# An attention block with modulation on one core: scale mods as rows, batch-1 transposes ahead of V, row-tiled text keys, output weights in row chunks

## The chip, the cores and the metric

One core of a Trainium2 chip. The metric is the device time of one execution in microseconds; lower is better. It is about 1.8 us more than the span of the profile, which starts and ends with the program's own instructions. The kernel before took 121.41 us (median of 3 runs, 121.23 to 121.57). A difference is called faster or slower from 2% on.

## The reference

Two token streams, image (2 x 256 tokens) and text (2 x 32), of width D = 1152, are normalised, modulated by vectors made from `c`, attended over jointly with one head of width D, projected and gated:

```python
mod_i = (_silu(c) @ wmod_img).reshape(B, 6, 1, D)      # shift, scale, gate are used; the same for text
hi = _layernorm(x_img) * (1 + sci) + shi               # ht likewise
qkvi, qkvt = hi @ wqkv_img, ht @ wqkv_txt
q, k, v = [concatenate([text, image], axis=1)]         # 288 tokens per batch
p = _softmax(einsum('bqd,bkd->bqk', q, k) * D ** -0.5)
a = einsum('bqk,bkd->bqd', p, v)
out_i = x_img + gai * (ai @ wo_img)                    # out_t likewise
```

Each of the 14 weight blocks is 1152 x 1152 in bf16, 2592 KB.

## The kernel before

The parts that the change touches; cuts are marked with `...`. `P` is 128, `KT` is 9 (rows of 128 of a weight block), `NTOK` is 288. TensorE runs its matmuls in the order of the program, as the chain of waits in the prediction shows. A **dummy** is a matmul whose result is never read.

```python
    for r0, r1 in ((0, 1), (1, 3), (3, 6), (6, KT)):              # V's weights, rows in four pieces
        nc.sync.dma_start(w_v_i[:, r0:r1, :], v_v[:, r0:r1, :])
    ...
    w_o_i = load_w(3, wo_img, 0)                                   # one DMA for the whole block
    ...
    def warm_up(n):                                                # dummies: their result is never read
        for _ in range(n):
            mm(wps[:], lhsT=warm[:, 0:P], rhs=warm[:], start=True, stop=True)
    warm_up(8)
    ...                                                            # transposes of silu(c)
    warm_up(17)
    ...
    def sc_cols(r0, r1):                                           # scale of the image, as columns
        ...
        for kt in range(r0, r1):
            for j in range(KT):
                mm(sc_ps[:, j, :], lhsT=w_sc_i[:, kt, j * P:(j + 1) * P], rhs=sT[:, kt, :], ...)
    ...                                                            # x normalised, 18 transposes of batch 0
    sc_cols(0, 4)
    warm_up(5)
    sc_cols(4, 7)
    out01 = x_transposes(0, 1)                                     # six transposes of batch 1
    sc_cols(7, K8)
    sc_cols(K8, KT)
    out31 = x_transposes(3, 1)
    out01()
    x_scale(0, 3, 0, sc_ps)                                        # VectorE, scale read from PSUM
    ...
    v_open(A0, 0, 3)                                               # V, four accumulators, rows 0 to 2
    out61 = x_transposes(6, 1)
    ...
    v_open(A1, 0, 3)
    v_open(A0 + A1, 3, KT - 2)
    ...
    def attn_out(b, d0=0, d1=KT):
        for dt in range(d0, d1):
            aps = ps_mm.tile([P, NTOK], f32, tag="mm")             # six PSUM buffers
            for kj in range(3):                                    # two blocks of image keys, one of text
                lhsT = v_i[...] if kj < 2 else v_t[...]            # text: 64 of 128 rows are zeros
                mm(aps[:], lhsT=lhsT, rhs=pT[:, kj, :], start=(kj == 0), stop=(kj == 2))
            ...                                                    # eviction, VectorE and ACT in turn

    v_txt()
    scores_txt()
    scores_img(0)
    img_gate()
    scores_img(1)
    p_transposes(0)
    txt_gate()
    attn_out(0, 0, 5)
    p_transposes(1)
    attn_out(0, 5, KT)
    attn_out(1)
```

## Time and profile before

| | before |
|---|---|
| time, median of 3 | 121.41 us |
| span of the profile | 119.5 us |
| TensorE busy | 114.6 us (96%) |
| DMA | full from 3 to 98.6 us |

The page's main lines and the chain of waits stand in the prediction. One more line of that chain serves below as the **mark** at which the front of the kernel is over, the first matmul of the image shift, which follows 63 matmuls of V (columns: start, length, what):

```profile
28.89 1.22 PE gps L61 x36
```

### The profile page before, as it was taken

Reading aid. Unit: us, or ns where it says so; the run is one execution under the profiler, and the core shown is the slowest. Engines: PE = TensorE matmul, PEld = TensorE weight load, DVE = VectorE, ACT = ScalarE, POOL = GpSimd, SP = SyncE. Lnnn points to the kernel's source line nnn. Section 1 sums busy time; section 2 is a strip of 40 time slices with the busy share of each in tenths; the row PEclk is TensorE's granted clock in tenths of the full one; section 3 lists DMA queues with packets and bytes.
Section 4 is the critical chain, followed back from the end, with each engine's and each line's share of the span. In section 5 each row is a group of like instructions: output and inputs, shape, how many; then the busy total and the mean of one; then the engine's idle time right before and its main releaser. Section 6 shows DMA issues by size and latency. Waiting matters only on the chain.

```text
span 119.5 us, 2609 instructions
## 1 busy us (share of the span) xinstructions
PE 114.6 (96%) x1105; PEld 67.2 (56%) x1105; DVE 74.1 (62%) x155; ACT 42.2 (35%) x86; POOL 11.6 (10%) x34
## 2 busy tenths in 40 slices
PE   5999999999999999999999999999999999999980
PEld 2248754445574444445444467886777866567660
DVE  1678292053866899999999700017785756666670
ACT  5799402031761424323039132335347610000000
POOL 8240000000000000000000000000211807100000
PEclk9999999999999999999999999999999999999999
DMA  3999999999999999999999999999999992620222
GB/s 136 379 383 396 403 404 411 415 408 414 405 398 400 401 413 411 411 413 410 415 403 410 413 413 411 406 411 405 413 417 397 411 370 81 148 99 0 99 68 80
DMA packets 18517, 40.86 MB, mean 342 GB/s; under 512 B 923, under 2 KB 1451, under 8 KB 18507
## 3 DMA queue, kind: packets, MB, share of 16 engines
q1 hardware_dynamic: 17632, 39.56, 84.9%
q0 software_dynamic: 480, 0.89, 2.5%
q10 hardware_dynamic: 395, 0.26, 0.7%
q8 instruction: 8, 0.13, 0.4%
q14 instruction: 2, 0.02, 0.0%
HBM read 39.38 MB, written 1.34 MB: 341 GB/s over the span
## 4 chain that ended last, share of the span: by engine, by line
PE 95%; DVE 2%; issue 0%; DVEq 0%
PE ps L61 52%; PE vps L61 15%; PE wps L61 8%; PE aps L61 6%; PE gps L61 6%; PE sps L61 4%; PE sc_ps L61 2%; PE tp L64 1%; PE pT_ps L64 1%; DVE tmp L615 1%; DVE o L616 0%; PE tpt L64 0%; DVE hS_i L240 0%; DVE warm L128 0%; PE sT_ps L64 0%
## 5 line engine op out<-in xcount | busy, mean ns | idle before, releaser
L61 PE MATMUL ps<-xT_i,t 128*128 128x512 bf16 x162 | 35.8, 379 | 0.0
L61 PEld LDWEIGHTS <-t 128*128 128x128 bf16 x405 | 22.8, 98 | 19.4 <-issue 0.7
L398 DVE SCALAR_TENSOR_TENSOR acc_sh<-t,sTf,acc_sh 128x1152 f32<-128x1152 bf16 x16 | 21.3, 1405 | 0.0
L61 PE MATMUL ps<-t,aT 128*128 128x384 bf16 (+3 forms) x153 | 20.2, 308 | 0.0
L61 PE MATMUL vps<-t,hS_i 128*128 128x512 bf16 (+1 forms) x108 | 18.1, 326 | 0.1
L61 PEld LDWEIGHTS <-aT 128*128 128x128 bf16 (+1 forms) x153 | 13.0, 101 | 7.1 <-issue 0.5
L61 PEld LDWEIGHTS <-hS_i 128*128 128x128 bf16 x108 | 8.9, 98 | 8.6 <-DVE hS_i L240 0.3
L61 PE MATMUL wps<-warm 128*128 128x512 bf16 x30 | 9.8, 491 | 1.2 <-DVE warm L128 1.2
L615 DVE TENSOR_TENSOR tmp<-ps,gb 128x384 bf16<-128x384 f32 (+2 forms) x13 | 6.8, 526 | 6.4 <-PE ps L61 5.2
L348 ACT ACTIVATE qkT<-ps 128x512 bf16<-128x512 f32 (+2 forms) x11 | 6.2, 563 | 12.3 <-PE ps L61 12.3
L483 POOL DMA_DIRECT2D mod_scratch<-g_sb x4 | 2.5, 634 | 78.3 <-ACT g_sb L173 78.3
L350 ACT CAST qkT<-ps 128x512 bf16<-128x512 f32 (+2 forms) x11 | 5.9, 554 | 8.5 <-PE ps L61 8.5
L171 DVE CAST v_i<-vps 128x512 bf16<-128x512 f32 x5 | 3.5, 692 | 7.6 <-PE vps L61 7.6
L171 DVE CAST v_t<-ps 64x288 bf16<-64x288 f32 x2 | 0.9, 460 | 11.7 <-ACT v_t L173 11.7
L61 PE MATMUL aps<-pT,v_i 128*128 128x288 bf16 x36 | 6.7, 287 | 0.0
L61 PEld LDWEIGHTS <-warm 128*128 128x128 bf16 x30 | 3.3, 117 | 5.9 <-issue 3.3
L587 DVE TENSOR_SCALAR aT<-aps,svc 128x288 bf16<-128x288 f32 x9 | 4.7, 518 | 2.4 <-PE aps L61 2.3
L61 PE MATMUL sps<-qkT 128*128 128x288 bf16 (+1 forms) x54 | 5.5, 287 | 0.0
L589 ACT ACTIVATE aT<-aps,svc 128x288 bf16<-128x288 f32 x9 | 4.5, 501 | 2.5 <-PE aps L61 2.5
L61 PE MATMUL aps<-pT,v_t 128*128 128x288 bf16 x18 | 5.1, 286 | 0.0
L61 PE MATMUL gps<-t,sT 128*32 128x288 bf16 x144 | 5.1, 287 | 0.0
L61 PE MATMUL ps<-hT_t,t 128*128 128x64 bf16 x162 | 5.1, 193 | 0.0
(106 smaller groups left out, 108.8 us busy)
## 6 DMA issues: line engine op xcount, KB each, us to landing
t<-in_wqkv_txt_dram SPq DMA_DIRECT2D x3, 2592.0 KB, 15.9
t<-in_wmod_img_dram SPq DMA_DIRECT2D x2, 2592.0 KB, 17.0
t<-in_wqkv_img_dram SPq DMA_DIRECT2D x2, 2592.0 KB, 20.3
t<-in_wmod_txt_dram SPq DMA_DIRECT2D x2, 2592.0 KB, 15.0
t<-in_wmod_txt_dram SPq DMA_DIRECT2D x3, 864.0 KB, 16.2
t<-in_wo_img_dram SPq DMA_DIRECT2D x1, 2592.0 KB
t<-in_wo_txt_dram SPq DMA_DIRECT2D x1, 2592.0 KB, 20.1
t<-in_wqkv_img_dram SPq DMA_DIRECT2D x2, 864.0 KB, 13.9
```

Source lines behind the costliest of these rows:

```text
L61: return pin(nc.tensor.matmul(*a, **k))
L64: return pin(nc.tensor.transpose(*a, **k))
L171: nc.vector.tensor_copy(out_ap, in_ap)
L348: nc.scalar.mul(out_ap, in_ap, SCALE)
L350: nc.scalar.copy(out_ap, in_ap)
L398: pin(eng.scalar_tensor_tensor(acc[:, b, :], w[:, kt, :], sTf[:, kt, b:b + 1], acc[:, b, :], op0=ALU.mult, op1=ALU.add))
L483: nc.gpsimd.dma_start(gsc[si, b, :].rearrange("(g j) -> g j", g=NGG), g_sb[b:P:32, :])
L587: nc.vector.tensor_scalar(dst, aps[:], bias, None, op0=ALU.add)
L589: nc.scalar.activation(dst, aps[:], ACT.Identity, bias=bias)
L615: nc.vector.tensor_mul(tmp[:, 0:n], ps[:, 0:n], gb[:, b, c0:c0 + n])
```

## The change

Its intent: take dummies off TensorE's path, let V start without transposes in between, have the text keys of two output tiles run side by side, let text V cover the softmax, and let the output projection start on part of its weights. `tile_position` makes a matmul use a part of TensorE's 128 x 128 array, here 32 columns or 64 rows of it; going from one such division to another is a change of **tiling mode**. The scale is said below to be in **column form** before the change and in **row form** after it.

```diff
-    for r0, r1 in ((0, 1), (1, 3), (3, 6), (6, KT)):
+    for r0, r1 in ((0, 1), (1, 2), (2, 3), (3, 5), (5, 7), (7, KT)):
...
-    w_o_i = load_w(3, wo_img, 0)          # and w_o_t
+    w_o_i = load_rows(3, wo_img, 0)       # three DMAs each
...
-    nc.vector.memset(warm[:], 0.0)
+    nc.vector.memset(warm[:], 1.0)
...
-    warm_up(17)
+    warm_up(14)
...
-            for j in range(KT):
-                mm(sc_ps[:, j, :], lhsT=w_sc_i[:, kt, j * P:(j + 1) * P], rhs=sT[:, kt, :], ...)
+            for g in range(NGG):          # four 32-column tiles, 288 columns each
+                mm(sc_ps[LW * g:LW * g + LW], lhsT=sT32[:, kt, :], rhs=group(w_sc_i, kt, g), ...,
+                   tile_position=(0, LW * g))
...
-    sc_cols(0, 4); warm_up(5); sc_cols(4, 7)
+    sc_rows(0, 4); warm_up(3); sc_rows(4, 7); warm_up(1)
...
+    sc1_i = mod_cols_of(sc_ps, "scc")     # VectorE's 32x32 block transpose
     out01()
-    x_scale(0, 3, 0, sc_ps)
+    x_scale(0, 3, 0)
+    out61 = x_transposes(6, 1)
     v_open(A0, 0, 3)
-    out61 = x_transposes(6, 1)
...
+        nc.vector.tensor_copy(v_t[64:64 + NTT, :], v_t[0:NTT, :])     # text V a second time
...
+    def attn_pair(ids0, ids1):            # two groups of three output tiles
+        attn_keys(t0, True)               # image keys of the first group
+        for n, key in enumerate(...):     # six text matmuls, t0 and t1 in turn
+            r0 = 64 * (n % 2)
+            mm(..., lhsT=v_t[r0:r0 + 64, ...], rhs=pTs[b][r0:r0 + 64, 2, :],
+               start=first, stop=not first, tile_position=(r0, 0))
+        attn_evac(t0); attn_keys(t1, False); attn_evac(t1)
...
-    v_txt()
     scores_txt(); scores_img(0); img_gate(); scores_img(1)
+    v_txt()
     p_transposes(0); txt_gate()
-    attn_out(0, 0, 5); p_transposes(1); attn_out(0, 5, KT); attn_out(1)
+    attn_pair(G[0], G[1]); p_transposes(1); attn_pair(G[2], G[3]); attn_pair(G[4], G[5])
```

More of the change, by code (lines that the diff above doesn't have):

```diff
@@ L120 @@
     w_ga_t = load_w(2, wmod_txt, 2 * D)
-    w_o_i = load_w(3, wo_img, 0)
-    w_o_t = load_w(1, wo_txt, 0)
+    w_o_i = load_rows(3, wo_img, 0)
+    w_o_t = load_rows(1, wo_txt, 0)
     nc.scalar.preload_act_table_set("natural_log_exp_and_others")
@@ L127 @@
     warm = const.tile([P, 512], bf)
-    nc.vector.memset(warm[:], 0.0)
-    unit = const.tile([P, P + B * KT], bf)
-    nc.gpsimd.memset(unit[:, 0:P], 1.0 / P)
-    nc.gpsimd.memset(unit[:, P:], 1.0)
+    nc.vector.memset(warm[:], 1.0)
+    NGG = 4
+    LW = P // NGG
+    unit = const.tile([P, LW], bf)
+    nc.vector.memset(unit[:], 1.0 / P)
     ident = const.tile([P, P], bf)
@@ L207, with group, mod_cols_of, sc_rows @@
     xT_i = act.tile([P, KT, B * NI], bf)
-    sc1_i = const.tile([P, KT, B], f32)
     qkT = act.tile([P, 2 * KT, B, NTOK], bf, tag="Q")
-    sc_ps = ps_mm.tile([P, KT, B], f32, tag="mm")
-    def sc_cols(r0, r1):
+    def group(w, kt, g):
+        return w[:, kt, :].rearrange("p (c g l) -> p g c l", g=NGG, l=LW)[:, g]
+    def mod_cols_of(gps, name):
+        t = const.tile([P, KT, LW], f32, name=name, tag={"shtc": "scc", "sctc": "shc"}.get(name, name))
+        pin(nc.vector.transpose(t[:].rearrange("p c l -> p (c l)"), gps[:].rearrange("p c l -> p (c l)")))
+        return t
+    sc_ps = ps_mm.tile([P, KT, LW], f32, tag="mm")
+    def sc_rows(r0, r1):
         if r0 == 0:
-            mm(sc_ps[:].rearrange("p kt b -> p (kt b)"), lhsT=unit[:, 0:P], rhs=unit[:, P:],
-               start=True, stop=False, skip_group_check=True)
+            for g in range(NGG):
+                mm(sc_ps[LW * g:LW * g + LW].rearrange("p c l -> p (c l)"), lhsT=unit[:], rhs=warm[:, 0:KT * LW],
+                   start=True, stop=False, tile_position=(0, LW * g))
         for kt in range(r0, r1):
-            for j in range(KT):
-                mm(sc_ps[:, j, :], lhsT=w_sc_i[:, kt, j * P:(j + 1) * P], rhs=sT[:, kt, :],
-                   start=False, stop=(kt == KT - 1), skip_group_check=True)
+            for g in range(NGG):
+                mm(sc_ps[LW * g:LW * g + LW], lhsT=sT32[:, kt, :], rhs=group(w_sc_i, kt, g),
+                   start=False, stop=(kt == KT - 1), tile_position=(0, LW * g))
     def x_transposes(k0, b):
@@ L235, in x_transposes, with x_scale @@
         return copy_out
-    def x_scale(k0, k1, b, sc=None):
-        sc = sc1_i if sc is None else sc
+    def x_scale(k0, k1, b):
         for kt in range(k0, k1):
             pin(nc.vector.tensor_scalar(hS_i[:, kt, b * NI:(b + 1) * NI], xT_i[:, kt, b * NI:(b + 1) * NI],
-                                        sc[:, kt, b:b + 1], None, op0=ALU.mult))
+                                        sc1_i[:, kt, b:b + 1], None, op0=ALU.mult))
     VW = 512
@@ L280 @@
         out()
-    sc_cols(0, 4)
-    warm_up(5)
-    sc_cols(4, 7)
+    sc_rows(0, 4)
+    warm_up(3)
+    sc_rows(4, 7)
+    warm_up(1)
     out01 = x_transposes(0, 1)
-    sc_cols(7, K8)
-    sc_cols(K8, KT)
+    sc_rows(7, K8)
+    sc_rows(K8, KT)
     out31 = x_transposes(3, 1)
+    sc1_i = mod_cols_of(sc_ps, "scc")
     out01()
-    x_scale(0, 3, 0, sc_ps)
-    pin(nc.vector.tensor_copy(sc1_i[:], sc_ps[:]))
+    x_scale(0, 3, 0)
+    out61 = x_transposes(6, 1)
     v_open(A0, 0, 3)
-    out61 = x_transposes(6, 1)
     out31()
@@ L301 @@
     v_open(A0 + A1, KT - 2, KT, kt_major=False)
-    NGG = 4
-    LW = P // NGG
-    def group(w, kt, g):
-        return w[:, kt, :].rearrange("p (c g l) -> p g c l", g=NGG, l=LW)[:, g]
     def mod_rows_of(w, lhs):
@@ L315, in mod_rows_of @@
         return gps
-    def mod_cols_of(gps, name):
-        t = const.tile([P, KT, LW], f32, name=name)
-        nc.vector.transpose(t[:].rearrange("p c l -> p (c l)"), gps[:].rearrange("p c l -> p (c l)"))
-        return t
     v_open([(2, 1)], 0, KT)
@@ L367 @@
     v_t = act.tile([P, D], bf)
-    nc.gpsimd.memset(v_t[NTT:P, :], 0.0)
     svr = act.tile([P, KT, LW], bf)
@@ L532, in softmax_tile @@
         for r0, r1, b in parts:
-            nc.vector.tensor_scalar_mul(pb[r0:r1, NI + NT * b:NI + NT * (b + 1)], e[r0:r1, NI:NTOK], rs[r0:r1, :])
+            nc.vector.tensor_scalar_mul(pb[r0:r1, NI:PBW].rearrange("p (h b n) -> p b h n", h=2, b=B)[:, b],
+                                        e[r0:r1, NI:NTOK].unsqueeze(1).to_broadcast([r1 - r0, 2, NT]), rs[r0:r1, :])
         pbs[key] = pb
@@ L576, in p_transposes, with attn_keys, attn_evac @@
         pTs[b] = pT
-    def attn_out(b, d0=0, d1=KT):
-        pT = pTs[b]
-        for dt in range(d0, d1):
-            aps = ps_mm.tile([P, NTOK], f32, tag="mm")
-            for kj in range(3):
-                lhsT = v_i[:, b * TPB + kj, dt * P:(dt + 1) * P] if kj < 2 else v_t[:, dt * P:(dt + 1) * P]
-                mm(aps[:], lhsT=lhsT, rhs=pT[:, kj, :], start=(kj == 0), stop=(kj == 2))
+    def attn_keys(tiles, first):
+        for b, dt in tiles:
+            for kj in range(2):
+                mm(tiles[(b, dt)][:], lhsT=v_i[:, b * TPB + kj, dt * P:(dt + 1) * P], rhs=pTs[b][:, kj, :],
+                   start=(first and kj == 0), stop=(not first and kj == 1))
+    def attn_evac(tiles):
+        for b, dt in tiles:
             dst, bias = aT[:, dt, b * NTOK:(b + 1) * NTOK], cols["v"][:, dt, b:b + 1]
             if evac_idx[0] % 2 == 0:
-                nc.vector.tensor_scalar(dst, aps[:], bias, None, op0=ALU.add)
+                nc.vector.tensor_scalar(dst, tiles[(b, dt)][:], bias, None, op0=ALU.add)
             else:
-                nc.scalar.activation(dst, aps[:], ACT.Identity, bias=bias)
+                nc.scalar.activation(dst, tiles[(b, dt)][:], ACT.Identity, bias=bias)
             evac_idx[0] += 1
-    v_txt()
+    def attn_pair(ids0, ids1):
+        t0 = {key: ps_mm.tile([P, NTOK], f32, tag="mm", name="aps") for key in ids0}
+        attn_keys(t0, True)
+        t1 = {key: ps_mm.tile([P, NTOK], f32, tag="mm", name="aps") for key in ids1}
+        for n, key in enumerate([x for pair in zip(t0, t1) for x in pair]):
+            first = key in t1
+            r0, (b, dt) = 64 * (n % 2), key
+            mm((t1 if first else t0)[key][:], lhsT=v_t[r0:r0 + 64, dt * P:(dt + 1) * P],
+               rhs=pTs[b][r0:r0 + 64, 2, :], start=first, stop=not first, tile_position=(r0, 0))
+        attn_evac(t0)
+        attn_keys(t1, False)
+        attn_evac(t1)
     scores_txt()
@@ L596 @@
     scores_img(1)
+    v_txt()
     p_transposes(0)
     txt_gate()
-    attn_out(0, 0, 5)
+    G = [[(b, dt) for dt in range(d0, d0 + 3)] for b in range(B) for d0 in range(0, KT, 3)]
+    attn_pair(G[0], G[1])
     p_transposes(1)
-    attn_out(0, 5, KT)
-    attn_out(1)
+    attn_pair(G[2], G[3])
+    attn_pair(G[4], G[5])
     def out_img(i, chunks, parts=None):
```

## The prediction

> **What bounds the kernel now.** I read the page's busy shares and slices first, then the chain of work that ended last, then the timeline of the first 18 us and of the attention, then the times of the DMAs from issue to landing.
>
> ```profile
> span 119.5 us, 2609 instructions
> PE 114.6 (96%) x1105; PEld 67.2 (56%) x1105; DVE 74.1 (62%) x155; ACT 42.2 (35%) x86; POOL 11.6 (10%) x34
> ...
> DMA  3999999999999999999999999999999992620222
> ...
> PE 95%; DVE 2%; issue 0%; DVEq 0%
> ```
>
> TensorE is 95% of the chain, so a microsecond of its stream that goes is a microsecond of the span, unless a wait replaces it. Beside it stands a second stream: DMA is at 9 from slice 2 to slice 33, that is up to 98.6 us (slices of 2.99 us). The 14 weight blocks come one after another; what each needs to land does not move when TensorE gets faster.
>
> The chain in order of time, cut to the stretches that the change touches (start, length, what):
>
> ```profile
> 1.23 3.59 PE wps L61 x8
> 4.82 0.12 PE sT_ps L64
> 4.94 4.94 PE wps L61 x17
> 9.88 1.00 PE tp L64 x18
> 10.88 0.90 PE sc_ps L61 x37
> 11.79 1.10 PE wps L61 x5
> 12.89 0.65 PE sc_ps L61 x27
> ...
> 14.44 0.30 DVE hS_i L240
> ...
> 17.55 0.34 PE tp L64 x6
> ...
> 83.29 1.22 PE gps L61 x36
> 84.51 2.31 PE sps L61 x18
> ...
> 91.06 4.88 PE aps L61 x39
> ```
>
> The wps pieces are dummy matmuls that keep TensorE busy while the norm of x is made; they stand in its program order, so they are on the path although they compute nothing. The first slab of normalised x is ready at 8.31 (timeline: its DVE row starts at 7.75 and takes 0.56), yet the transposes start at 9.88: the dummies overshoot by 1.5 us. The attention (aps) is pure matmul issue: in the timeline one output tile (three 288-column matmuls) follows the last every 0.37 us, 0.123 us per matmul.
>
> **What the Trainium skill says.** (1) "TensorEngine Tiling (Array Packing)", Key Properties: a change of tiling mode drains TensorE. The trace agrees: the 36 gate matmuls on 32-column tiles run four at a time, 9 x 0.123 = 1.11, and took 1.22; the 18 score matmuls after them 18 x 0.123 = 2.21, and took 2.31. So **a switch costs about 0.1 us**. (2) "TensorE: Matmul & The Clock Gate", Part 3: matmuls on different row strips run at the same time. No row-tiled pair stands in this trace; the column tiles, four at a time above, agree in kind. (3) The same page, Part 1: the clock doubles after some microseconds of activity, on a free-running window. The trace agrees: dummy weight loads are 0.43 us apart until 7.0 us and 0.20 from 7.3. (4) "VectorE: DVE Perf Modes", Zero memsets can be issued as uint32 (trn2): a memset takes one cycle per element, and only zero may be written as words. The trace has the zero memset of the dummies' operand as 256 words in 0.27 us; the new one, of ones, is built as 512 elements.
>
> **The change, part by part.**
>
> *Dummies and front.* The memset of ones takes about 2 x 0.27, so TensorE starts 0.27 later, at 1.50. The block of 17 dummies becomes 14: 3 x 0.213 (the warm spacing) = 0.64 less. Net, if the clock's step moves along with the start: 9.88 - 0.64 + 0.27 = 9.51; if it stays where it is in time, half of the delay is won back and it is 9.35. I take 9.4. That is still after 8.31, so no wait.
>
> From there, on TensorE: 18 transposes 1.00 -> 10.40. The scale mods change shape: 81 full-array matmuls with 2 columns plus one, at 24 ns each (0.90 + 0.65 + 0.44 = 1.99 us in all), become 36 + 4 on 32-column tiles with 288 columns, 40/4 x 0.123 = 1.23 us. But they are now in another tiling mode than the transposes and dummies around them: three pieces, six switches, 0.6. So 1.83 for 1.99: nearly even. Laid out: switch and 20 matmuls 0.71 -> 11.11; switch and 3 dummies 0.74 -> 11.85; switch and 12 matmuls 0.47 -> 12.32; switch and 1 dummy 0.31 -> 12.63; six transposes 0.34 -> 12.97; switch and 8 matmuls 0.34 -> 13.3. The weights are there: the last row of the scale block was issued at about 3.3 and landed 9.2 later, at 12.5; the first row of V at 3.83 + 9.5 = 13.3.
>
> Then VectorE. Before, it scaled straight from PSUM: matmuls done 14.34, scale 14.44 + 0.30, V at 14.79. Now a 32x32 block transpose of 128x288 comes in between; its four like ones in the page took 0.47 to 0.48 us. 13.3 + 0.1 + 0.48 + 0.30 + 0.05 = **14.25**. The last six batch-1 transposes, now ahead of V, need the buffer that ACT's copy (0.80 us) of the group before frees: 12.97 + 0.05 + 0.80 = 13.82, plus 0.34 = 14.2. Both arrive together, so this move costs nothing there and takes the 0.34 at 17.55 out of the V stream. V's second group starts at 14.25 + 12 x 0.2155 = 16.84; before, it was 17.72. **Front: 0.88 us gained.** V's rows come in smaller pieces so that they are there: rows 3 to 5 landed at about 5.1 + 13.3 = 18.4 and would now be wanted at 16.84 + 6 x 0.2155 = 18.1; the smaller piece should land one row (0.7 us) earlier.
>
> *Middle.* Nothing is removed from 17 to 77 us. In VectorE's order the text scale's transpose moves behind the shift's, some 0.6 + 0.76 us more after the shift rows; before, the text rows were modulated at 68.56 and wanted at 70.86, so it fits.
>
> *Text V behind the scores.* Same matmuls (77.62 to 80.19, 2.57 us), later, one switch more: 0.1 lost, and about 0.1 won, since the wait for the first pT (0.31 before attention, most of it the switch) goes.
>
> *Attention.* 18 matmuls of the text keys, 64 of whose 128 rows were zeros, become 9 pairs on 64-row tiles: 9 x 0.123 = 1.10 saved. Each of the three pairs of groups goes into the 64-row mode and back: 6 x 0.1 = 0.6 lost. Eviction: six tiles of 0.50 to 0.52 us on two engines, 1.55 per 1.9 us of TensorE, and all six PSUM buffers are in use; that fits narrowly. But the second pair of groups now starts with batch 1 and wants the second pT at once; its copy on ACT took 0.88 and stands behind evictions, so 0.1 to 0.2 of wait. **Attention: 1.10 - 0.6 - 0.1 = 0.4.**
>
> *Output weights in row chunks.* The output projection begins at 95.78 without a wait. The gate blocks landed at 62.86 + 16.1 = 79.0 and 73.41 + 12.2 = 85.6, so the image output block is due at about 92.1 (estimate: one block each 6.5 us). It will be wanted at 95.78 - 1.3 = 94.5, so chunks are worth nothing by themselves. Its text counterpart is issued later, behind text V at about 85.5, but still ahead of 92.1, and is wanted near 107.
>
> Sum: 0.88 + 0.4 = 1.3 us. 121.41 - 1.3 = **120.1 us**.
>
> **The rivals.** *A, the weight stream becomes the bound.* For it: DMA is full to 98.6 us, and moving text V behind the scores pulls the image gate forward, from 83.22 to 83.22 - 0.88 - 2.57 = 79.8, where its weights land at 79.0; the text gate comes at 86.4, weights 85.6. Margins of 0.8 us. Against: positive still, and the gaps between landings are even. If the front won 1.3 or more, this would cap it: not under 119.4. If the stream slips by 1 us, 0.3 is lost: 120.4.
>
> *B, the drains eat the pairs.* If a switch into row tiles is 0.18 us rather than 0.1, or the pairs don't overlap, or the six PSUM buffers stall (0.2 per group pair), attention gives nothing: 120.5 to 120.8. For it: TensorE moves directly between all six PSUM buffers. Against: each eviction has about 1.2 us of TensorE work before its buffer is wanted.
>
> *C, the front only trades.* If TensorE at the front waits for something that I have not seen (the two casts of the silu that the 32-column form needs, the block transpose, a later clock step; at 0.43 for 0.21 us per dummy, one step a window late costs over 1 us), 0.5 or less remains: 120.8 or worse.
>
> *D, drains are free in part* (weights of the next mode loaded ahead): up to 0.6 more in front and 0.6 in attention: 118.9 at the best, but then A takes some back.
>
> **Range and chances.** D and A together put the low end at 119.3; B or C alone put it at 120.8, so 119.3 to 120.9. Over 2% faster means under 118.98: it needs D nearly whole and no stall from A: 0.10. Slower by 2% (over 123.8) needs a clock step lost and stalls at once: 0.02. Within 2%: 0.88.
>
> **What the profile after would show.** Right: first dummy at about 1.5; transposes at 9.4; V at 14.2 with the last batch-1 transposes just ended; the gates beginning at 79.8 and 86.4 without a DMA wait; nine text-key pairs whose starts are 0.12 apart by the pair, with a gap of 0.2 instead of 0.12 around each block; attention, from first aps to first output matmul, 6.8 us instead of 7.24; TensorE still above 94% of the chain. Wrong: a wait for DMA in front of a gate (A); attention at 7.2 or more, or a wait of aps for an eviction (B); V at 14.7 or later (C); six switches in front that show less than 0.05 us each (D).

## More of the kernel before

A term used from here on: the **tail** is the time from the end of the last VectorE result to the end of the span. In the kernel before that result ends at 116.47 + 0.23 = 116.70, and the tail is 2.78 us.

## The result, and the profile after

| | before | after |
|---|---|---|
| time, median of 4 | 121.32 us | 120.38 us (120.09 to 120.71) |
| ratio, 95% interval | | 0.9922 (0.9892 to 0.9951) |
| span of the profile | 119.5 us | 118.6 us |

Executions over 1.5% slower than the fastest of the same kernel are left out of the means. A ratio here and below is the mean time of one kernel's runs over that of the other's of the same rounds, so not quite the ratio of the medians. It says 0.95 us less: "same" by the 2% rule, and clear of noise. The prediction was 120.1, range 119.3 to 120.9: right as a whole. Step by step it is less right, and that is the subject of the rest.

First the page and the chain by line of the kernel after:

```profile
span 118.6 us, 2515 instructions
PE 112.1 (95%) x1051; PEld 64.0 (54%) x1059; DVE 75.3 (63%) x157; ACT 41.8 (35%) x86; POOL 10.3 (9%) x31
...
PE 86%; DMA 8%; DVE 2%; SPq 1%; issue 1%; DVEq 0%
```

TensorE is 86% of the chain for 95%, and 8% have gone to DMA. The chain in order of time shows where:

```profile
2.12 9.85 DMA t<-in_wmod_img_dram
11.97 0.04 issue
12.01 0.55 PE sc_ps L61 x12
...
13.83 0.49 DVE scc L217
...
14.42 0.30 DVE hS_i L248
...
14.76 2.12 PE vps L61 x9
...
28.53 1.22 PE gps L61 x36
```

The dummies are gone from the chain. In their place stands the landing of rows 4 to 6 of the scale weights at 11.97; then come matmuls, block transpose, first scale and V in series. V starts at 14.76, where 14.25 was predicted, and the front's mark moves from 28.89 to 28.53: 0.36 us won for 0.88 predicted. Of these, 0.33 come from the six transposes that left V's stream (from V's first matmul to the mark 14.10 us before, 13.77 after), and only 0.03 from V's start. The wait itself, in the timeline (start, length, ..., in brackets idle time before and its releaser):

```profile
12.01 0.55 PE L61 MATMUL sc_ps<-t,sT 128*32 128x288 bf16 x12 [0.52 <-DMA t<-in_wmod_img_dram]
```

A shorter wait behind it, which the chain doesn't name, is the one that sets V's start: the last scale row, issued at 3.65, landed at 13.43 (from the landings in the packed trace), and its four matmuls start at 13.48, 0.33 us after those of the row before, where two such groups follow each other in 0.12.

The attention, in the timeline of the kernel after:

```profile
88.32 0.91 PE L61 MATMUL aps<-pT,v_i 128*128 128x288 bf16 x6
89.17 0.54 PE L61 MATMUL aps<-pT,v_t 64*128 64x288 bf16 x6
89.64 0.91 PE L61 MATMUL aps<-pT,v_i 128*128 128x288 bf16 x6
...
91.83 0.72 PE L61 MATMUL aps<-pT,v_t 64*128 64x288 bf16 x6
92.47 1.64 PE L61 MATMUL aps<-pT,v_i 128*128 128x288 bf16 x12
...
95.27 1.95 PE L61 MATMUL ps<-t,aT 128*128 128x384 bf16 x11
```

The pairs do run side by side: the full-array matmuls follow the six text matmuls after 0.47 us (89.17 to 89.64), where six one after another would need 0.74. The six full-array matmuls before them need 0.74 (6 x 0.123) and the text starts after 0.85: the switch costs 0.11. The second text block takes 0.64 until the next start instead of 0.47: it waits 0.17 for the second pT, as predicted. From the first aps matmul to the first output matmul 6.95 us, for 7.24 before (88.54 to 95.78).

The text V move cost something. From the end of the text queries and keys to the first aps matmul it was 77.62 to 88.54, 10.92 us; it is 77.26 to 88.32, 11.06 us.

The last term nobody had predicted. The last VectorE result comes 0.51 us earlier (115.96 + 0.23 = 116.19 for 116.70), but the span is 0.87 shorter (119.48 and 118.61 in the packed traces): the tail is 2.43 us instead of 2.78. What SyncE did after the last transfer had landed shows in a view of the closing instructions, by engine, with the count behind the x, first for the kernel before (118.2 to 118.7 us), then for the kernel after (117.7 to 118.0 us):

```profile
L669 SPq EVENT_SEMAPHORE  x7: 27/28/28, 118.2 to 118.6; - x7
```

```profile
L683 SPq EVENT_SEMAPHORE  x1: 28/28/28, 117.7 to 117.7; - x1
```

At the end of the program SyncE waits for the completion semaphores of the transfers one after another in a fixed order, 0.06 us each when nothing is to be waited for. Before, the last transfer to land was on a semaphore that stands early in this order, so six more waits followed it (118.23 to 118.60); after, it is on the last, and none follows. (The packed traces show it: the order is 100, 102, 104, 106 to 110; the last transfer to land signals 102 before and 110 after.) The semaphores go round the transfers in turn; the change issues six more of them, so the last ones fall on others.

So in this pair of profiles: front 0.36 + attention 0.29 - text V 0.14 + tail 0.35 = 0.86 of 0.87 us.

### The profile page after: what moved, and what is told of

It reads as the page before. It is cut to its first block, busy times and chain, and to the rows that moved or that the text cites. A ratio compares the mean times of both kernels' runs of the same rounds, so it can differ in the third digit from the quotient of the medians.

```text
span 118.6 us, 2515 instructions
## 1 busy us (share of the span) xinstructions
PE 112.1 (95%) x1051; PEld 64.0 (54%) x1059; DVE 75.3 (63%) x157; ACT 41.8 (35%) x86; POOL 10.3 (9%) x31
## 4 chain that ended last, share of the span: by engine, by line
PE 86%; DMA 8%; DVE 2%; SPq 1%; issue 1%; DVEq 0%
PE ps L61 52%; PE vps L61 15%; DMA t<-in_wmod_img_dram 8%; PE gps L61 6%; PE aps L61 6%; PE sps L61 5%; PE sc_ps L61 1%; PE pT_ps L64 1%; SPq L104 1%; DVE tmp L629 1%; DVE o L630 0%; DVE scc L217 0%; SPq L108 0%; PE tpt L64 0%; PE tp L64 0%
## 5 line engine op out<-in xcount | busy, mean ns | idle before, releaser
L61 PEld LDWEIGHTS <-t 128*128 128x128 bf16 x324 | 20.4, 98 | 19.2 <-issue 0.7
L61 PE MATMUL wps<-warm 128*128 128x512 bf16 x25 | 7.7, 458 | 1.6 <-DVE unit L132 1.5
L61 PEld LDWEIGHTS <-sT 128*32 128x32 bf16 x180 | 4.5, 96 | 2.8 <-issue 2.2
L174 ACT CAST v_i<-vps 128x512 bf16<-128x512 f32 x4 | 2.3, 580 | 10.0 <-PE vps L61 10.0
L61 PEld LDWEIGHTS <-warm 128*128 128x128 bf16 x26 | 2.6, 111 | 5.2 <-issue 2.1
L61 PE MATMUL aps<-pT,v_i 128*128 128x288 bf16 x36 | 5.3, 288 | 0.0
## 6 DMA issues: line engine op xcount, KB each, us to landing
t<-in_wmod_txt_dram SPq DMA_DIRECT2D x3, 864.0 KB, 14.7
```

The lines of the kernel that those rows point to most:

```text
L61: return pin(nc.tensor.matmul(*a, **k))
L174: nc.scalar.copy(out_ap, in_ap)
```

## The experiments

Twelve runs were made, all with correct results, in three lots, the first on chip 2 and the others on chip 4 (the record names no chip for the first comparison); each ratio is to the kernel before in the same lot (medians 121.25, 121.47 and 121.14).

### Both kernels again

No edit.

> The kernel before, unchanged, for a second profile and the spread. Theory (the front is now tied to the landing of the scale weights): its ratio to itself is 1.00 within 0.3%; its second V group starts near 17.7 us whenever the rows landed, since here TensorE's own queue of dummies is the later one. Rival (run-to-run luck: the clock step fell at 7.2 us in the kernel before and at about 5 us in the kernel after): the clock step moves by microseconds between two profiles of the same kernel, and the span with it, by up to half of that.

Measured: ratio 1.0007 (0.9985 to 1.0029). The clock did step earlier than in the first profile: the dummies after the first eight took 4.48 us instead of 5.00, and V started at 14.39 instead of 14.79. But the mark of the front stayed, 28.91 for 28.89. The timeline shows why:

```profile
14.39 1.04 PE L61 MATMUL vps<-t,hS_i 128*128 128x512 bf16 x3
...
15.68 1.89 PE L61 MATMUL vps<-t,hS_i 128*128 128x512 bf16 x8 [0.26 <-DVE hS_i L240]
```

V ran its first row (four matmuls; the records of a few matmuls are missing, so x3) and then stood until 15.68. The view names VectorE, which had finished the first three hS_i rows at 14.73. What else these matmuls wait for is the DMA piece with rows 1 and 2 of V's weights, and the packed trace settles it: that piece landed at 15.64. Two more kernels with the old pieces do the same: landed 15.43, V goes on at 15.47 (attention only); 16.14 and 16.18 (output weights). In the first profile of before it landed at 14.88, ahead of need. V's start was no longer held by the dummies either, but by the last scale row, which landed at 13.51. So with 0.4 us fewer of dummies the kernel before won nothing: behind the dummies stood a DMA wait that ends at nearly the same time.

> The changed kernel, unchanged. Theory: ratio 0.992 (0.989 to 0.995) again, and again a wait for rows 4 to 6 of the scale weights (0.5 us in the first profile) ahead of the scale matmuls; V starts between 14.3 and 14.8 depending on when the last row lands. Rival (the late landing of x and of the scale rows, 0.5 and 0.9 us later than in the profile of before, was an accident of that one profile): V starts at 14.25 as predicted and the ratio is nearer 0.989.

Measured: ratio 0.9936 (0.9912 to 0.9961). V at 14.64, after a wait of 0.35 for rows 4 to 6; mark at 28.41. The first theory stands, the rival falls: the rows landed 9.7 to 10.5 us after their issue in this profile and in all eleven others of the experiments, and 9.9 in the first of after. It was the first profile of **before**, with 9.0, from which the prediction read its landings, that was the odd one out.

The landings in the packed traces say more: it is the last scale row that binds. In all seven profiles with the row form its matmuls start 0.04 us after it has landed, and in the five of them with one block transpose V starts 1.33 us after that landing, whatever the dummies did: 13.43 and 14.76 in the first profile of after, 13.31 and 14.64 in this one, 14.07 and 15.40 with the dummies put back. Where the column form waits for the same row, V starts 0.88 us after it (13.51 and 14.39 in again before; also in V's rows and output weights).

### The two large parts apart

Front only: the edit is the diff above without its attention, text V and output weight parts. Attention only: those parts without the output weights.

> The front part alone: scale mods as rows, fewer dummies, last batch-1 transposes ahead of V, V rows in finer pieces; attention, text V and output weights as before. By the first two profiles the front gives 0.36 us (first gate-shift matmul at 28.53 for 28.89): ratio 0.997. By the prediction it gives 0.88: ratio 0.993.

> The attention part alone: text keys in row-tiled pairs, text V behind the scores; front and output weights as before. From the two profiles it gives 0.2 to 0.3 us (from the end of the text queries and keys to the first output matmul): ratio 0.998. By the prediction 0.4: 0.997. If the pairs gave all of their 1.1 us: 0.991.

Measured: front only 0.9963 (0.9938 to 0.9987), so 0.45 us; attention only 0.9981 (0.9961 to 1.0002), so 0.23 us, not clear of zero by itself. In the profile of front only the mark is at 28.37 (0.52 earlier) and the tail 2.68; in that of attention only the time from the end of the text queries and keys to the last VectorE result shrank by 0.15 us (39.08 to 38.93: attention 0.29, less 0.14 for text V), and the tail is 2.79. Both times fit the smaller of the expected sizes; the profile of attention only lies below the 0.2 to 0.3 expected. Together they are 0.68 of 0.78 to 0.95; the rest should be the output weights' chunks.

### V's rows, and the output weights, each alone

```diff
 # v_rows_only: the kernel before, and
-    for r0, r1 in ((0, 1), (1, 3), (3, 6), (6, KT)):
+    for r0, r1 in ((0, 1), (1, 2), (2, 3), (3, 5), (5, 7), (7, KT)):
 # wo_rows_only: the kernel before, and
-    w_o_i = load_w(3, wo_img, 0)
-    w_o_t = load_w(1, wo_txt, 0)
+    w_o_i = load_rows(3, wo_img, 0)
+    w_o_t = load_rows(1, wo_txt, 0)
```

> The kernel before with one line of the change: V's first rows in six pieces instead of four. In the second profile of the kernel before, V's fifth matmul, the first on row 1, waited until 15.68 though TensorE was free at 15.25, for the piece with rows 1 and 2. Theory (the front of the kernel before is bound by that piece, not by the dummies): the wait goes, the first gate-shift matmul moves from 28.9 to about 28.4 to 28.6, ratio 0.997, most of what the whole front part gave. Rival (the dummies are the path, as predicted): nothing moves, 28.9, ratio 1.00.

> The kernel before with the output weights in row chunks and nothing else. TensorE does not wait for these weights in any profile, so its stream must not change: output projection at 95.8, last VectorE result at 116.7. Theory (the tail, from the last VectorE result to the end of the span, depends on which completion semaphores the last transfers use, and four more transfers shift those): the tail is not 2.78 us as in both profiles of before but nearer the 2.42 of both profiles of after; ratio 0.997 to 0.998. Rival (the tail differs for another reason, such as the clock or the timing of the text output): tail 2.78, ratio 1.000.

Measured: V's rows 0.9956 (0.9937 to 0.9975), 0.53 us (0.30 to 0.77, 0.10 of it tail): as much as the whole front part, by one line. The profiled run doesn't show it in the mark (28.92): in that run the last scale row landed late, TensorE waited 0.32 for it, and V started at 14.81. But V's first twelve matmuls then ran without the stop after the fourth. The fair profile to set beside it is that of the output weights, the same front with the old pieces and with rows that landed as late. There V starts at 14.89, stops, and reaches the mark at 29.41, 0.49 us later than with the finer rows:

```profile
14.89 1.04 PE L61 MATMUL vps<-t,hS_i 128*128 128x512 bf16 x3
...
16.18 1.89 PE L61 MATMUL vps<-t,hS_i 128*128 128x512 bf16 x8 [0.26 <-DVE hS_i L240]
```

So the finer rows take away a stop of 0.22 to 0.43 us where the weights land late (the three profiles of the old pieces that show it); in the first profile of before, where they landed early, there is no stop to take away.

Output weights 0.9967 (0.9946 to 0.9988), 0.40 us, in a kernel in which TensorE never waits for these weights. Its tail is 2.54 instead of 2.78 us, and in its trace two closing waits follow the landing of the last transfer; with V's rows in six pieces four follow, and the tail is 2.68. That is what four and two more transfers should do to the turn of the semaphores:

| kernel | transfers more than before | closing waits after the last landing | tail |
|---|---|---|---|
| before, again before, attention only, dummies only | 0 | 6 | 2.78, 2.78, 2.79, 2.79 us |
| V's rows, front only, fewer dummies | 2 | 4 | 2.68 us each |
| output weights | 4 | 2 | 2.54 us |
| after, again after, the four made from it | 6 | 0 | 2.43 to 2.44 us |

0.06 us a wait through the whole table. It explains 0.24 of the 0.40 us of the output weights; the interval of that run, 0.15 to 0.66 us, holds 0.24, and nothing in its profile speaks for more.

### The dummies

```diff
 # dummies_only: the kernel before, and          # fewer_dummies: also V's rows in six pieces
-    warm_up(17)
+    warm_up(14)
-    sc_cols(0, 4); warm_up(5); sc_cols(4, 7)
+    sc_cols(0, 4); warm_up(3); sc_cols(4, 7); warm_up(1)
```

> The kernel before with fewer dummies alone (17 to 14, 5 to 3 and 1 later), scale mods still as columns, V rows in the old pieces. The prediction counted the three dummies of the first block as 0.64 us of the path. Theory (V's rows 1 and 2 bind the front): V starts earlier, about 14.0, but its fifth matmul still waits until 15.5 to 15.7; gate-shift at 28.7 to 28.9, ratio 0.999 to 1.000. Rival: V starts at 14.0 and all of it follows: 28.3, ratio 0.995.

> Fewer dummies and the finer V rows together, scale mods still as columns and the last batch-1 transposes still inside V. Theory (what now sets V's start in the changed kernel is the landing of the last scale row at 13.3, then 0.24 us of matmuls and 0.6 us of block transpose that the column form doesn't need): V starts at about 14.0 instead of 14.6, the gate-shift at 28.2 or earlier even with 0.34 of transposes inside V, against 28.4 with the whole front part: ratio 0.995. Rival (the row form and the moved transposes are what gained): 28.6 or later, 0.997.

Measured: dummies only 1.0020 (0.9994 to 1.0047), its six runs in two clusters, 121.4 to 121.5 and 122.1 to 122.2; the first three, picked after the fact, average 121.45 for 121.57 of the kernel before, which is the theory's 0.999. Fewer dummies with finer rows: three runs at 120.7 to 120.9 (0.9942) and three at 122.9 to 123.0. Neither theory had this. The table by stretch of dummies only tells it; the columns are the stretch, its length, busy time and instructions of TensorE, its weight loads, VectorE, ACT and GpSimd, then the granted clock (the share of TensorE's full clock that it was given), the DMA share and GB/s:

```profile
11.00:12.00 1.00, 0.59 (x2) 0.10 (x1) 1.00 (x3) 0.97 (x4) 0.00 (x0) 1.00 1.06 399
12.00:13.00 1.00, 0.91 (x29) 0.79 (x30) 0.45 (x1) 0.69 (x1) 0.00 (x0) 1.00 1.02 383
13.00:14.00 1.00, 1.00 (x27) 1.00 (x26) 0.00 (x0) 0.44 (x1) 0.00 (x0) 0.66 1.04 406
14.00:15.00 1.00, 1.00 (x7) 0.66 (x7) 0.91 (x5) 0.36 (x1) 0.00 (x0) 0.50 1.04 410
```

The granted clock fell to half from 13 to 17 us, in the middle of V's start; in the profile of fewer dummies, one of its slow runs, from 11 to 17.4. The kernel after, with as few dummies, kept its clock in the same stretches, although TensorE is no busier there:

```profile
11.00:12.00 1.00, 0.49 (x2) 0.09 (x1) 0.96 (x2) 0.97 (x3) 0.00 (x0) 1.00 1.04 401
...
13.00:14.00 1.00, 0.98 (x17) 0.54 (x15) 0.17 (x1) 0.74 (x1) 0.00 (x0) 1.00 1.05 408
```

It kept it in all six profiles of kernels with fewer dummies and the row form, and the mean granted clock of their 34 runs is 0.994 or more, for 0.968 to 0.984 in the six long runs here. So the dummies had a use beyond filling a wait, and **something in the front part lets them go**. That it is the row form is likely and not shown: the columns' matmuls move 2 columns each and the rows' 288, so the array does far less in the same busy time, which would fit, but with the row form came dummies of ones for zeros, a first dummy 0.26 us later, the moved transposes and other places of the gaps, and no run separates these.

```diff
 # dummies_back: the kernel after, and
-    warm_up(14)
+    warm_up(17)
-    sc_rows(0, 4); warm_up(3); sc_rows(4, 7); warm_up(1)
+    sc_rows(0, 4); warm_up(5); sc_rows(4, 7)
```

> The changed kernel with its dummies put back (17 and 5 instead of 14, 3 and 1). The prediction's largest term was three dummies fewer, 0.64 us. Theory (TensorE waits for the scale rows anyway, 0.35 to 0.52 us in the two profiles of the changed kernel, so the dummies fill a wait): V starts at most 0.2 later, ratio 0.992 to 0.995, as the changed kernel. Rival (they are on the path): V starts 0.6 to 0.8 later, ratio 0.998 to 1.000.

Measured: 0.9954 (0.9926 to 0.9982), between the two theories, and too wide to tell 0.2 us from nothing. In its profile, the slowest of its six runs, V starts at 15.40, as late as the rival had it, but the dummies are not the reason:

```profile
14.11 0.31 PE L61 MATMUL sc_ps<-t,sT 128*32 128x288 bf16 x4 [0.23 <-DMA t<-in_wmod_img_dram]
```

TensorE waited 0.23 for the last scale row, which landed at 14.07 in this run, and V follows that landing by the same 1.33 us as in the kernel after. So in this profile the dummies put back cost nothing; where the row lands earlier they may, and the times leave that open. The 0.64 of the prediction is not shown.

### What a switch of tiling mode costs

```diff
 # nine_blocks: the kernel after, and in attn_pair
-        six text matmuls in one block; then attn_keys(t1, False)
+        for k0, k1 in zip(t0, t1):
+            two text matmuls, rows 0 and 64
+            attn_keys({k1: t1[k1]}, False)
```

> The changed kernel with each text-key pair in a block of its own, so nine blocks of row tiles instead of three: same matmuls, twelve more switches of tiling mode. Theory (a switch costs 0.1 us also between full-array and row-tiled matmuls): from the start of the first aps matmul to the first output matmul 6.95 + 12 x 0.1 = 8.1 to 8.2 us, ratio to before 0.993 + 0.010 = 1.003. Rival (what held the attention back was evictions or the late second pT, not the switches): 7.0 to 7.3 us, ratio 0.993 to 0.996.

Measured: ratio 1.0062 (1.0034 to 1.0089), so all of the gain and more is lost. In its timeline:

```profile
89.13 0.30 PE L61 MATMUL aps<-pT,v_t 64*128 64x288 bf16 x2
89.36 0.42 PE L61 MATMUL aps<-pT,v_i 128*128 128x288 bf16 x2
89.71 0.30 PE L61 MATMUL aps<-pT,v_t 64*128 64x288 bf16 x2
```

A pair and the two image matmuls behind it take 89.13 to 89.71, 0.58 us: three slots of 0.123 are 0.37, and the two switches take 0.21. From the first aps to the first output matmul it is 8.22 us for 6.95 (88.29 to 96.51): 1.27 / 12 = **0.106 us per switch**. The theory stands.

### A faster version

```diff
 # split_turn: the kernel after, and
-    sc1_i = mod_cols_of(sc_ps, "scc")
+    sc_turn(0, 3)                  # block transpose of the columns that V reads first
     out01()
     x_scale(0, 3, 0)
+    sc_turn(3, KT)
 # split_turn_pt: also
     p_transposes(0)
+    p_transposes(1)
     txt_gate()
     attn_pair(G[0], G[1])
-    p_transposes(1)
```

> The changed kernel with the block transpose of the scale columns split: the three columns blocks that V's first scales read first, the other six after those scales. Theory (between the last scale row and V stand matmuls, block transpose and the first scale in series): the first transpose takes about 0.2 instead of 0.48, V starts 0.2 to 0.3 earlier (it is then held by the last batch-1 transposes, whose PSUM buffer the ACT copy frees), ratio 0.991. Rival (V's rows hold it): no change, 0.993.

> The same with the transposes of batch 1's probabilities ahead of the text gate instead of between the attention groups, so that the second pT is ready when the second pair of groups wants it. Theory: the six text matmuls of that pair take 0.54 instead of 0.72 us, and attention as a whole (without the transposes, which move in front of it) 0.2 less; ratio 0.0015 to 0.002 below that of the run with the split transpose alone, about 0.989. Rival (the ACT copy then delays the text V evictions and the gain is lost): the same ratio as that run.

Measured: split 0.9920 (0.9892 to 0.9947); with the early transposes 0.9897 (0.9867 to 0.9927), median 119.92, the fastest of all. The first block transpose takes 0.28 us instead of 0.48, and V starts 1.41 us after the last scale matmuls begin (13.12 to 14.53), 1.61 with the whole one (nine blocks: 13.12 to 14.73); from the landing of the last row it is 1.13 in both split kernels, for 1.33. The text matmuls that waited for the second pT now run as the others, in the timeline of the last kernel:

```profile
91.98 0.54 PE L61 MATMUL aps<-pT,v_t 64*128 64x288 bf16 x6
92.45 1.64 PE L61 MATMUL aps<-pT,v_i 128*128 128x288 bf16 x12
```

0.47 us from start to start, for 0.64. The steps of 0.2 us are shown in the profiles; by times alone the two kernels are not apart from each other or from the kernel after, since the intervals overlap.

Not tried: putting all attention matmuls into 64-row tiles, which would take the six switches away. Two row tiles of one output tile would then write one PSUM bank with nothing to order them, which "TensorEngine Tiling (Array Packing)", Gotcha 1, rules out.

## Why the prediction was right, and where it was not

The sum was 1.3 us; 0.95 and 0.78 were measured. By its steps:

- **Front, 0.88: too large.** Profiles give 0.36 and 0.50, the front alone 0.45 in times with 0.10 of tail in it. The 0.88 was 0.34 for the transposes that leave V's stream and 0.54 for V's earlier start. The first came true (0.33). The second did not: V starts 0.03 us earlier in the first pair of profiles and 0.25 later in the second (14.39 to 14.64). The step that failed is "The weights are there". The prediction put the landing of the last scale row at 12.5, from one profile, and did not check rows 4 to 6. In the 13 later profiles that row landed at 13.27 to 14.07, and in the kernel after V follows it by 1.33 us. With this falls the reading of the chain in the kernel before. The dummies stood in front of landings that end at nearly the same time, and the chain of waits shows only the last of two such things: in the second profile the dummies were 0.5 us shorter and the kernel not faster, since V then waited for its rows 1 and 2. What removes that wait is the finer pieces of V's rows (0.42 in the second pair: 0.33 + 0.42 - 0.25 is its 0.50), a line that the prediction counted as a mere precaution. Rival C (the front only trades) was closer than the main line, and its sign, V at 14.7 or later, was met in the first profile.
- **Scale rows for columns, "nearly even": not where the weights bind.** From the landing of the last row to V it is 1.33 us with rows and 0.88 with columns, so there the row form loses 0.45. It may have another use, which the prediction did not see: with columns and fewer dummies the clock is lost in the profiles and in about half of the runs, with rows in none.
- **Attention, 1.10 - 0.6 - 0.1 = 0.4: right in each term.** Six switches at 0.106 are 0.64, the wait for the second pT was 0.17, the pairs overlap: 0.29 measured.
- **Text V, 0.1 lost and 0.1 won: mis-sized.** It lost 0.14. Most of the earlier wait for the first pT had been the switch, as the prediction itself said, so there was little to win.
- **Output weights, "worth nothing by themselves": wrong.** 0.35 us of tail come with their four transfers and the two more of V's rows. No view that the prediction used reaches past the last result.
- **Rivals A and D** are not borne out: no gate waited for its weights, and the switches cost their full 0.1. One of the named signs of being right failed: TensorE was to stay above 94% of the chain, and has 86%.

So the front was 0.5 us too large and attention with text V 0.25, and the missing tail made up 0.35 of it. The total is right partly by luck, because errors cancelled.

## What to carry to other kernels

Work that pads a wait looks like the path in a chain of waits; before counting its removal as a gain, look for the next thing that ends at nearly the same time, and take DMA landings from several profiles. Padding on TensorE may also be keeping its clock, so look at the granted clock stretch by stretch after thinning it, and at every run, not at the median. And a change that only alters the number of DMAs can move the end of a kernel by tenths of a microsecond.

## What the Trainium skill lacked or had wrong

- "TensorEngine Tiling (Array Packing)", Key Properties, says that a change of mode drains TensorE and gives no size. Here it is 0.106 us per switch between full-array and 64-row matmuls of 288 columns (1.27 us for twelve), and 0.1 for 32-column tiles.
- "TensorE: Matmul & The Clock Gate", Part 1, has the clock fall after an idle window of about 3.4 us, and adds under a second failure mode that frequent short idles can do it too, without their lengths. Here it fell to half for one stretch of 3.41 us after no wait above 0.42 us (dummies only, TensorE busy 0.59 to 1.00 of each of the four microseconds before) and for 6.83 us after one of 0.86 and one of 0.42 (fewer dummies); both have 2-column matmuls there, and the kernels with 288-column ones kept their clock after waits of up to 0.90.
- None of its pages that I read tells that the closing waits of a program go through the transfers' completion semaphores one by one, 0.06 us each, so that the tail depends on which one the last transfer uses: 2.78, 2.68, 2.54 and 2.43 us with 6, 4, 2 and 0 waits behind it.
- "VectorE: DVE Perf Modes", Zero memsets can be issued as uint32 (trn2), gives one cycle per element. The zero memset took 0.27 us for 256 words, and that of ones 0.48 for 512 elements, somewhat less than the 0.53 that the page's 0.96 GHz gives.
